# Linear attention and a cosine FFN on one core: the first 512 tokens taken from all four sequences instead of two

## The chip, the core and the metric

The kernel runs on one core of a Trainium2 chip. The core has a matmul engine (TensorE, PE in the profile), a vector engine (VectorE, DVE), an activation engine (ScalarE, ACT), a general engine (GpSimd, POOL) and a queue engine (SyncE, SP) that only issues DMAs. Sixteen DMA engines move data between the device memory and the core's on-chip memory. The metric is the device time of one execution in microseconds; lower is better. The profile shows one execution, and its span runs from the first to the last instruction.

## What is computed

For each of 4 sequences and 8 heads, with 768 tokens and head size 64, a linear attention with decay is computed in blocks of 64 tokens. Its output, 3072 tokens by 512, goes through an FFN with the gate h * cos(h):

```python
for b in range(nb):                                   # nb = 12 blocks of 64 tokens
    intra = einsum('bhic,bhjc->bhij', qb, kb) * Dmask
    intra = einsum('bhij,bhjd->bhid', intra, vb)
    inter = einsum('bhid,bhde->bhie', qb * lam_pow, kv_state)
    out[:, :, sl] = intra + inter
    kv_state = lam_block * kv_state + einsum('bhsd,bhse->bhde', kb * rev_pow, vb)
x = out.transpose(0, 2, 1, 3).reshape(3072, 512)
h = x @ w_in                                          # 512 x 2048
return (h * cos(h)) @ w_out                           # 2048 x 512
```

What matters below: the state of a sequence runs through its tokens in order, and different sequences have nothing to do with each other.

## The kernel before

**Blocks and pairs.** The 3072 tokens are 24 blocks of 128 (P). The function `where(n)` says which sequence and which chunk of it block n is. Two blocks of two sequences are worked on together as a pair. The first four blocks (SPANS = 2, so 2 * SPANS blocks) are special: a "span" x is 256 successive tokens of sequence x, that is its chunks 0 and 1. Token 2u + s lies on partition u with s beside it, so a span fills 128 partitions, chunk 0 the lower 64 of them (rows `halves[0]`) and chunk 1 the upper 64. After the spans come pairs 2 to 5 with chunks 2 to 5 of sequences 0 and 1, and pairs 6 to 11 with chunks 0 to 5 of sequences 2 and 3.

**A span (`add_span`).** Loads bring q and k as float32 by SP (`add_span_load`, tile `sp_f`) and v cast to bfloat16 by POOL (tile `v_sp`). `prep` scales q and k (DVE, for the second span's k POOL). TensorE transposes them, ACT copies the results out, TensorE forms the scores, DVE masks them (`scores_out`), and `values` multiplies with v. The second chunk of a span needs the state of the first: `update` (L631) makes it on TensorE, `update_out` copies it to `kv_bd` on ACT, and `carried` (L650) adds its part. `values_out` copies the attention output to `xT`, the input of the FFN. `add_span_state` (L705) then makes the state after both spans, 256 tokens, for pair 2: a PSUM result, a DVE copy (`sum`) and a POOL cast (`S`).

**A pair from 2 on.** `add_load` asks for q, k and v of both blocks (256 KB each, 1024 pieces of 256 bytes). POOL, DVE or ACT scale them (`prepare`). Up to pair 2 TensorE transposes; from pair 3 on (DMA_FROM = 6) SP issues two DMA transposes (L380). Then come scores (L422), update (L434), values (L484) and the part carried from the state (L516). A pair whose chunk is 0 has no carried part for its first half; the last pair of a group makes only one half of the update.

**The FFN (`add_ffn`).** Blocks are grouped in TILES of 4, 2, 2, 2, 2, 2, 2, 4 and 4. For each of the 16 slices of the hidden dimension there is a hidden matmul group (L738, 4 matmuls), a cosine on ACT (L744) and a product on DVE (L750, tile `g`). Then for each block four projection groups of four matmuls (L784) follow, a copy to `o_sb` and a store. A block of the first four stores its even and odd tokens apart, with two DMAs of 64 rows (L805); the others use one DMA of 128 rows (L807). All stores but the very last are on SP's queue.

**What sets the order.** `Planner.order` places every step by its assumed cost, its dependencies and a priority, and the instructions of each engine and queue are emitted in that order. Loads on SP follow the list `names`. Three links matter here. The load q of block 4, the first of pair 2 (the third pair), waits for the product of hidden slice KF - 3 = 13 of the first FFN tile (`pace`). The weights are loaded by POOL in pieces, w_in in six and w_out in four, the fourth w_out piece after q of block 4 has landed. And `keep_awake` puts idle matmuls into TensorE's gaps before the first FFN tile.

Of the kernel before, what the change touches and what calls it, by code (L numbers as in the profile page):

```python
# [10 lines left out]
F32 = mybir.dt.float32  # L11
BF16 = mybir.dt.bfloat16
# [6 lines left out]
SPANS = 2  # L19
# [15 lines left out]
STATE_OUT = [("ACT", "ACT"), ("ACT", "ACT")]  # L35
LATE = 30.0
ORDER = "q0 k0 q1 k1 v0 v1 i0 i1 i2 i3 i4 i5 o0 o1 o2 q4 q5 k4 k5 o3"

# [105 lines left out]
def kernel(  # L144
# [10 lines left out]
    nc = tc.nc  # L155
    B, H, S, D = q.shape
    P = 128
# [10 lines left out]
    def where(n):  # L168

        if n < 2 * SPANS:  # L170
            return n // 2, n % 2
        g, c = divmod(n // 2, NB)
        return 2 * g + n % 2, c

    BUFS = {"ld": 6, "qk": 3, "v_s": 6, "qkT": 3, "s_m": 4, "cos": 3, "o_sb": 4}
    ctx.enter_context(tc.manual_schedule())
# [6 lines left out]
    def bank(i, shape, dt, name):  # L183
        return psum.tile(shape, dt, tag=f"bank{i}", bufs=1, name=name)
# [6 lines left out]
    ident = consts.tile([P, P], BF16)  # L191
    make_identity(nc, ident)
    pos_sp = consts.tile([P, 2], F32)
    nc.gpsimd.iota(pos_sp, pattern=[[1, 2]], base=-S // 2, channel_multiplier=2,
                   allow_small_or_imprecise_dtypes=True)
    mask_sp = consts.tile([P, 2, P], F32)
    nc.gpsimd.memset(mask_sp, 1.0)
    for i in range(2):
# [10 lines left out]
    nc.vector.memset(halfpi, math.pi / 2.0)  # L209
    blank = consts.tile([P, 4 * P], F32)  # L210
    nc.vector.memset(blank, 0.0)  # L211
    kv_bd = consts.tile([P, 2, NP, P], BF16)
    nc.vector.memset(kv_bd, 0.0)
    lnl = consts.tile([P, H], F32)
    nc.scalar.activation(lnl, lam_bc, AF.Ln)
    expo_sp = consts.tile([P, H, 2], F32)
# [50 lines left out]
    def start(queue, o, x, deps):  # L267
        i = queue.dma_start(out=o, in_=x)  # L268
        for d in deps:
            tc.add_manual_dep(i.ins, d.issue.ins.ins.name, mybir.DependencyInfo(  # L270
                mybir.DependencyClass.Sync, mybir.DependencyReason.DATA), reason="order of loads")
        return i

    def add_span_load(name, src, x, prio, deps):
        def emit(_):
            if on_pool:
                t = span_v[x]
            else:
                if ("raw", x) not in live:
                    live["raw", x] = work.tile([P, 2, H, 2, D], F32, tag="g", name="sp_f")  # L280
                t = live[name, "sp", x] = live["raw", x][:, "qk".index(name[0])]
            return start(nc.gpsimd if on_pool else nc.sync, t.rearrange("u h s d -> u h (s d)"),
                         src[x, :, 0:2 * P, :].rearrange("h (u s) d -> u h (s d)", s=2), deps)

        on_pool = name == "v_f"
        issue, load_t[name, "sp", x] = dma("POOL" if on_pool else "SP", 1.5, 1.0 if on_pool else 0.5, emit, prio, deps,
                                           lat=0.95 if on_pool else 1.0)
        return load_t[name, "sp", x]

    def add_load(n, name, src, prio, deps=()):  # L290
        b, c = where(n)

# [10 lines left out]
        issue_t[name, n], load_t[name, n] = dma("SP", LOAD_US, 0.85, emit, prio, deps, get=name,  # L303
                                                lat=1.9 if name == "v_f" and n < 2 * SPANS + 2 else 1.0)
        return load_t[name, n]

    w_t, pace = {}, []
# [101 lines left out]
    def add_scores(pr, part):  # L409

        pa = lambda x: prio_attn(2 * pr, x)
        g, c = divmod(pr, NB)
        last, early = c == NB - 1, pr == SPANS
        nonlocal first_sum

# [57 lines left out]
    def add_stretch(pr):  # L473

        n0 = 2 * pr
        g, c = divmod(pr, NB)
        pa = lambda part: prio_attn(n0, part)
        tile_i, j0 = tile_of(n0)

# [96 lines left out]
        if (pr + 1, 1) in Uo:  # L576
            Uo[pr + 1, 1].deps.append(v2)
        for x, y in zip(chain, chain[1:]):
            x.then = y
# [5 lines left out]
    def add_span(x):  # L585
# [40 lines left out]
        def update(t):  # L626
            L["kv"] = bank(t.bank[0], [P, NP, P], F32, "ps_kv")
            rows = chunks[0][0]
            for p in range(NP):
                for s in range(2):  # L630
                    nc.tensor.matmul(L["kv"][:, p, :], lhsT=L["k"][rows, s, 2 * p:2 * p + 2, :], rhs=L["v"][rows, s, 2 * p:2 * p + 2, :],  # L631
                                     start=(p == 0 and s == 0), stop=True, skip_group_check=True)

        def update_out(_, h, e):
            (nc.scalar.copy if e == "ACT" else nc.vector.tensor_copy)(kv_bd[h, x, :, h], L["kv"][h, :, h])

        def values(task, hp):
            if hp == 0:
                L["o"] = [bank(i, [P, NP, P], F32, "ps_o") for i in task.bank]
            for p in range(2 * hp, 2 * hp + 2):  # L640
                for s in range(2):
                    for rows, c in chunks:
                        for i, h in enumerate(halves):
                            nc.tensor.matmul(L["o"][c][h, p, :], lhsT=L["v"][rows, s, 2 * p + i, :],  # L644
                                             rhs=L["s_m"][rows, i, p, s, :],
                                             start=(p == 0 and s == 0), stop=True, skip_group_check=True)

        def carried(_):
            for p in range(NP):
                nc.tensor.matmul(L["o"][1][:, p, :].rearrange("e (s u) -> e s u", s=2),  # L650
                                 lhsT=kv_bd[:, x, p, :], rhs=L["qT"][:, :, p, chunks[1][0]],
                                 start=False, stop=True, skip_group_check=True)

        def values_out(_, c, e):
            if ("xT", 0) not in live:
# [7 lines left out]
        for hp in range(2):  # L663
# [11 lines left out]
            s1 = pl.add("PE", 0.42, outs, partial(scores, hp=hp), pa(0.1 + 0.1 * hp), banks=2)  # L675
            if x and hp == 0:

                spans[0]["values"].deps.append(s1)
                s_first = s1
            so[hp] = [pl.add("DVE", 0.69, [s1], partial(scores_out, hp=hp, i=i), pa(0.1 + 0.1 * hp + 0.05 * i)) for i in range(2)]  # L680
            s1.bank_frees = [[t] for t in so[hp]]

        u = pl.add("PE", 0.42, v_t + kt + [spans[0].get("carried")], update, pv(0.1), banks=1)
        Uo_sp[x] = [pl.add(e, 0.4 if e == "ACT" else 0.42, [u], partial(update_out, h=h, e=e), pv(0.1))
                    for h, e in zip(halves, STATE_OUT[x])]
        u.bank_frees = [Uo_sp[x]]
        span_deps.extend(v_t + kt)
        v0 = pl.add("PE", 0.35, so[0] + v_t + [spans[0].get("carried")], partial(values, hp=0), pv(0.2), banks=2)
# [5 lines left out]
        L["update"], L["values"], L["carried"] = u, v0, second  # L694
        L["straight"] = v1

    def add_span_state():


        def update(t):  # L700
            live["kv", 1] = bank(t.bank[0], [P, H, D], F32, "ps_kv")
            for h in range(H):
                for s in range(2):
                    for L, r in zip(spans, halves):
                        nc.tensor.matmul(live["kv", 1][r, h, :], lhsT=L["k"][:, s, h, :], rhs=L["v"][:, s, h, :],  # L705
                                         start=(h == 0 and s == 0), stop=True, skip_group_check=True)

        def state(_):
            nc.vector.tensor_copy(new_sum(1, 1), live["kv", 1])  # L709

        def state_16(_):
            nc.gpsimd.tensor_copy(new_S(1, 1), live["sum", 1, 1])  # L712

        u = pl.add("PE", 16 * QUART + SW, span_deps + [w_t["out", 0]], update, LATE, banks=1)
        x = pl.add("DVE", 0.69, [u], state, LATE)
        Uo[1, 1] = pl.add("POOL", 0.61, [x], state_16, LATE)
        u.bank_frees = [[x]]

    h_last, o_last = {}, {}
    hid, closing = [], None  # L720
# [1 line left out]
    def add_ffn(i):  # L722
# [4 lines left out]
        for f in range(KF):  # L727
            gate[f] = []
            blocks = [(0, 2), (2, 4)] if i == 0 and f < SPLIT else [(0, nb)]
            for b0, b1 in blocks:  # L730
# [37 lines left out]
        for j in range(nb):  # L768
# [4 lines left out]
            for piece, part in enumerate(pieces):  # L773
# [26 lines left out]
                def store_out(_, eng, j=j, piece=piece, part=part, width=width):  # L800
                    b, c = where(n0 + j)
                    r0 = b * S + c * P
                    if n0 + j < 2 * SPANS:
                        for s, h in enumerate(halves):
                            nc.sync.dma_start(out=out[r0 + s:r0 + P:2, :], in_=live["o_sb", i, j, piece][h])  # L805
# [47 lines left out]
            pr += 1  # L853
        add_ffn(i)
    for f in range(2, SPLIT):
        hid[2 * f].deps.append(spans[1]["carried"])
    issue_t["q_f", 2 * SPANS].deps += pace
    closing.deps.append(v12[SPANS])
    first_sum.deps += Vo[2 * SPANS]
# [56 lines left out]
```

## Time and profile before

| | us |
|---|---|
| median of 3 runs | 204.16 (203.99 to 204.69) |
| the profiled execution | 204.18 |
| its span | 202.5 |
| TensorE busy | 193.8 |
| hidden matmuls (L738) | 90.5 |
| projection matmuls (L784) | 88.3 |
| TensorE's first hidden matmul starts at | 15.37 |
| TensorE's last matmul ends near | 199.6 |

The granted TensorE clock is full throughout. A mean of 168 GB/s goes through the DMA engines; the queue of SP takes 62.2% of the time of all sixteen, the queue of POOL 16.3%. The page's forty slices are of 5.06 us each. A digit in them is the busy share of a slice in tenths. In an "issue" row the time to landing counts from the issue.

The loads of q, k and v have a median of 3.9, 4.3 and 5.0 us to landing, a store of 256 KB 2.5 us, and a store of 128 KB (the halves of the first four blocks) 3.9 us.

### The profile page before, as it was taken

To read this page: it belongs to the slowest core of one execution; us is meant where nothing else is said; L and a number is where in the kernel's file an instruction comes from. 1 tells how busy PE (TensorE), PEld (TensorE's weight loads), DVE (VectorE), ACT (ScalarE), POOL (GpSimd) and SP (SyncE) were. 2 spreads that over 40 slices of the span, in tenths; PEclk is the share of its full clock that TensorE was granted. 3 is DMA by queue.
4 is the path that set the end of the run, shared out by engine and by line. 5 is a ranking of instruction groups with operands and counts; after the bars stand their busy time and mean duration, and the time that the engine had idled before them with its cause. 6 is when DMAs were issued, how large, how long until landed. Compare 5 with 4: busy or idle time off the path is not lost.

```text
span 202.5 us, 5913 instructions
## 1 busy us (share of the span) xinstructions
PE 193.8 (96%) x2441; PEld 116.4 (57%) x2469; DVE 116.6 (58%) x228; ACT 119.9 (59%) x240; POOL 64.7 (32%) x85
## 2 busy tenths in 40 slices
PE   6799999999999999999999999999999999999994
PEld 3367444547747858766658676755445444444443
DVE  2888774257954967858548575734579544444001
ACT  4978871228837878565639666654877554355120
POOL 5694004046245163544653272543510000000000
PEclk9999999999999999999999999999999999999999
DMA  4999999988889998999999999999920010111112
GB/s 117 324 189 206 202 204 217 184 191 217 188 212 239 241 217 195 229 157 254 254 254 186 237 236 154 256 146 273 234 68 3 3 52 0 52 55 52 52 52 104
DMA packets 96762, 33.94 MB, mean 168 GB/s; under 512 B 84320, under 2 KB 93792, under 8 KB 96736
## 3 DMA queue, kind: packets, MB, share of 16 engines
q1 hardware_dynamic: 89232, 28.78, 62.2%
q0 software_dynamic: 7360, 4.72, 16.3%
q8 instruction: 19, 0.31, 0.7%
q14 instruction: 7, 0.06, 0.1%
q10 hardware_dynamic: 144, 0.07, 0.1%
HBM read 27.27 MB, written 6.29 MB: 166 GB/s over the span
## 4 chain that ended last, share of the span: by engine, by line
PE 92%; DMA 3%; issue 2%; SPq 2%; POOL 1%; ACT 0%; POOLq 0%; ACTq 0%
PE ps_h L738 41%; PE ps_f L784 40%; DMA sp_f<-in_k_dram 3%; PE ps_o L484 2%; PE ps_s L422 2%; PE ps_kv L434 2%; PE ps_o L516 2%; SPq L268 1%; PE ps_o L644 1%; PE ps_kv L631 1%; POOL k_sp L599 1%; PE ps_x L484 0%; PE ps_t L374 0%; PE ps_t L607 0%; PE ps_s L618 0%
## 5 line engine op out<-in xcount | busy, mean ns | idle before, releaser
L750 DVE TENSOR_TENSOR g<-ps_h,cos 128x256 bf16<-128x256 f32 (+1 forms) x148 | 73.2, 503 | 42.9 <-ACT cos L744 42.0
L744 ACT ACTIVATE cos<-ps_h,halfpi 128x256 f32<-128x256 f32 (+1 forms) x148 | 75.7, 539 | 29.4 <-PE ps_h L738 28.6
L738 PE MATMUL ps_h<-xT,w_in_sb 128*128 128x256 bf16 (+1 forms) x586 | 90.5, 304 | 0.5 <-issue 0.3
L784 PE MATMUL ps_f<-w_out_sb,g 128*128 128x512 bf16 (+2 forms) x378 | 88.3, 370 | 2.0 <-issue 1.3
L738 PEld LDWEIGHTS <-w_in_sb 128*128 128x128 bf16 x592 | 57.1, 98 | 30.1 <-DVE xT L524 0.4
L784 PEld LDWEIGHTS <-g 128*128 128x128 bf16 x400 | 37.6, 98 | 37.2
L798 ACT COPY o_sb<-ps_f 128x512 f32<-128x512 f32 (+1 forms) x24 | 13.8, 573 | 29.7 <-PE ps_f L784 29.6
L344 POOL TENSOR_TENSOR qk<-q_f,q_scale 128x512 bf16<-128x512 f32 x19 | 19.6, 1045 | 36.4 <-DMA q_f<-in_q_dram 33.6
L352 POOL TENSOR_TENSOR v_s<-v_f,v_scale 128x512 bf16<-128x512 f32 x19 | 19.6, 1044 | 15.6 <-DMA v_f<-in_v_dram 12.6
L427 DVE TENSOR_TENSOR s_m<-ps_s,mask 128x512 bf16<-128x512 f32 x20 | 13.0, 685 | 3.6 <-PE ps_s L422 3.0
L348 POOL CAST qk<-k_f 128x512 bf16<-128x512 f32 x18 | 11.1, 614 | 11.0 <-DMA k_f<-in_k_dram 10.9
L524 ACT CAST xT<-ps_o 128x512 bf16<-128x512 f32 x11 | 6.0, 588 | 9.6 <-PE ps_o L516 6.3
L440 DVE TENSOR_TENSOR sum<-sum,ps_kv 128x512 f32<-128x512 f32 x15 | 10.2, 682 | 0.6
L445 ACT CAST S<-sum 128x512 bf16<-128x512 f32 x15 | 9.2, 617 | 0.9 <-DVE sum L440 0.8
L798 DVE COPY o_sb<-ps_f 128x384 f32<-128x384 f32 x1 | 0.6, 557 | 11.5 <-DMA out_dram<-o_sb 11.5
L484 PEld LDWEIGHTS <-v_s 64*64 64x64 bf16 x320 | 3.9, 107 | 4.1 <-issue 3.6
L876 PE MATMUL ps_idle<-blank 128*128 128x512 f32 (+2 forms) x8 | 4.7, 723 | 1.6 <-DVE blank L211 1.6
L623 DVE TENSOR_TENSOR s_m_sp<-ps_s,mask_sp 128x512 bf16<-128x512 f32 x8 | 5.1, 683 | 1.0 <-PE ps_s L618 1.0
L484 PE MATMUL ps_o<-s_m,v_s 64*64 64x64 bf16 x256 | 5.1, 196 | 0.1
L712 POOL CAST S<-sum 128x512 bf16<-128x512 f32 x1 | 0.6, 607 | 14.0 <-DVE sum L709 14.0
L501 DVE COPY spare<-ps_o 1x1 f32<-1x1 f32 x5 | 0.8, 156 | 7.3 <-PE ps_o L484 7.3
L535 DVE TENSOR_TENSOR xT<-ps_o,cross 128x256 bf16<-128x256 f32 x8 | 3.1, 422 | 2.9 <-PE ps_o L516 2.9
(74 smaller groups left out, 94.7 us busy)
## 6 DMA issues: line engine op xcount, KB each, us to landing
q_f<-in_q_dram SPq DMA_DIRECT2D x20, 256.0 KB, 3.9
k_f<-in_k_dram SPq DMA_DIRECT2D x20, 256.0 KB, 4.3
v_f<-in_v_dram SPq DMA_DIRECT2D x20, 256.0 KB, 5.0
out_dram<-o_sb SPq DMA_DIRECT2D x19, 256.0 KB, 2.5
w_out_sb<-in_moe_w_out_dram POOLq DMA_DIRECT2D x4, 512.0 KB, 12.8
sp_f<-in_q_dram SPq DMA_DIRECT2D x2, 512.0 KB, 6.2
sp_f<-in_k_dram SPq DMA_DIRECT2D x2, 512.0 KB, 5.6
w_in_sb<-in_moe_w_in_dram POOLq DMA_DIRECT2D x4, 256.0 KB, 6.9
```

What stands on the lines that cost most here:

```text
L344: vec[e].tensor_mul(new_qk()[:, 0, :, s], live.pop(("q_f", 2 * pr + s)), q_scale[:, c, :].unsqueeze(2).to_broadcast([P, H, D]))
L348: (nc.scalar.copy if early else nc.gpsimd.tensor_copy)(new_qk()[:, 1, :, s], live.pop(("k_f", 2 * pr + s)))
L352: vec[e].tensor_mul(live["v_s", 2 * pr + s], live.pop(("v_f", 2 * pr + s)), v_scale[:, c, :].unsqueeze(2).to_broadcast([P, H, D]))
L427: nc.vector.tensor_mul(t, live["s", pr][s], mask.unsqueeze(1).to_broadcast([P, H, D]))
L440: nc.vector.tensor_add(new, live["sum", pr, 0] if half else live["sum", pr - 1, 1], live["kv", pr][half])
L445: nc.scalar.copy(new_S(pr, half), live["sum", pr, half])
L484: yield lambda h=h: nc.tensor.matmul(o[halves[h % 2], h // 2], lhsT=live["v_s", n0 + s][m, h, :], rhs=live["s_m", n0 + s][m, h, :], start= ...
L738: nc.tensor.matmul(t[:, :n], lhsT=w_in_sb[:, kd, f * P:(f + 1) * P], rhs=live["xT", i][:, kd, at], start=(kd == 0), stop=(kd == KD - 1))
L744: nc.scalar.activation(c[:, :n], live["h", i, f, at.start][:, :n], AF.Sin, bias=halfpi)
L750: return nc.vector.tensor_mul(live["g", i][:, f, at], live.pop(("h", i, f, at.start))[:, :n], live.pop(("c", i, f, at.start))[:, :n])
L784: nc.tensor.matmul(live["f", i, j, piece][:, :width], lhsT=live["g", i][:, f, j * P:(j + 1) * P], rhs=w_out_sb[:, f, part], start=(f == 0) ...
L798: (nc.scalar.copy if eng == "ACT" else nc.vector.tensor_copy)(o[:, :width], live["f", i, j, piece][:, :width])
```

## The change

The first four blocks are now the first chunks of all four sequences. `where` gives blocks 0 to 3 the sequences 0, 1, 3 and 2 with chunk 0. A span's lower 64 partitions hold one sequence and its upper 64 another, so nothing is carried within a span: `update`, `update_out`, `carried` and `kv_bd` go. The span loads become two DMAs of 64 partitions each, as the halves now come from two sequences. `pos_sp` counts each half from the same position. `add_span_state` makes two states, one for each group of two sequences (keys 1 and 6), with 64 matmuls of 64 rows for 32 of 128. The pairs are then 2 to 6 with chunks 1 to 5 of sequences 0 and 1, and 7 to 11 with chunks 1 to 5 of sequences 2 and 3, so every pair has a carried part. The load of the third pair waits for hidden slice KF - 5 = 11. The planner's assumed latency for early v loads is 1.4 for 1.9. The store of a block of the first four is one DMA whose DRAM side is ordered by odd and even tokens first.

```diff
@@ where
         if n < 2 * SPANS:
-            return n // 2, n % 2
-        g, c = divmod(n // 2, NB)
+            return (0, 1, 3, 2)[n], 0
+        g, c = group(n // 2)
         return 2 * g + n % 2, c
+    def group(pr):
+        g, c = divmod(pr - SPANS, NB - 1)
+        return g, c + 1
...
-    nc.gpsimd.iota(pos_sp, pattern=[[1, 2]], base=-S // 2, channel_multiplier=2,
-                   allow_small_or_imprecise_dtypes=True)
+    for i in range(2):
+        nc.gpsimd.iota(pos_sp[i * D:(i + 1) * D], pattern=[[1, 2]], base=-S // 2, channel_multiplier=2,
+                       allow_small_or_imprecise_dtypes=True)
...
-    kv_bd = consts.tile([P, 2, NP, P], BF16)
-    nc.vector.memset(kv_bd, 0.0)
...
@@ add_span_load
-            return start(nc.gpsimd if on_pool else nc.sync, t.rearrange("u h s d -> u h (s d)"),
-                         src[x, :, 0:2 * P, :].rearrange("h (u s) d -> u h (s d)", s=2), deps)
+            for i, u in enumerate(halves):
+                last = start(nc.gpsimd if on_pool else nc.sync, t[u].rearrange("u h s d -> u h (s d)"),
+                             src[where(2 * x + i)[0], :, 0:P, :].rearrange("h (u s) d -> u h (s d)", s=2), () if i else deps)
+            return last
...
@@ add_span
-        u = pl.add("PE", 0.42, v_t + kt + [spans[0].get("carried")], update, pv(0.1), banks=1)
-        Uo_sp[x] = [pl.add(e, 0.4 if e == "ACT" else 0.42, [u], partial(update_out, h=h, e=e), pv(0.1))
-                    for h, e in zip(halves, STATE_OUT[x])]
-        u.bank_frees = [Uo_sp[x]]
...
-        second = pl.add("PE", MM(P, 4) + 0.1, [v1] + Uo_sp[x], carried, pv(0.3))
-        for c, (t, e) in enumerate(zip((v1, second), VALUES_OUT[x])):
-            Vo[2 * x + c] = [pl.add(e, 0.6 if e == "ACT" else 0.69, [t], partial(values_out, c=c, e=e), pv(0.3) if c == 0 else -1200.0)]
+        for c, e in enumerate(VALUES_OUT[x]):
+            Vo[2 * x + c] = [pl.add(e, 0.6 if e == "ACT" else 0.69, [v1], partial(values_out, c=c, e=e), pv(0.3) if c == 0 else -1200.0)]
...
@@ add_span_state
+        keys = [SPANS - 1, SPANS + NB - 2]
         def update(t):
-            live["kv", 1] = bank(t.bank[0], [P, H, D], F32, "ps_kv")
+            for key, i in zip(keys, t.bank):
+                live["kv", key] = bank(i, [P, H, D], F32, "ps_kv")
             for h in range(H):
                 for s in range(2):
-                    for L, r in zip(spans, halves):
-                        nc.tensor.matmul(live["kv", 1][r, h, :], lhsT=L["k"][:, s, h, :], rhs=L["v"][:, s, h, :],
-                                         start=(h == 0 and s == 0), stop=True, skip_group_check=True)
+                    for x, (key, L) in enumerate(zip(keys, spans)):
+                        for c, rows in enumerate(halves):
+                            nc.tensor.matmul(live["kv", key][halves[where(2 * x + c)[0] % 2], h, :],
+                                             lhsT=L["k"][rows, s, h, :], rhs=L["v"][rows, s, h, :],
+                                             start=(h == 0 and s == 0), stop=True, skip_group_check=True)
...
+        for i, key in enumerate(keys):
+            x = pl.add("DVE", 0.69, [u], partial(state, key=key), LATE + 2 * i)
+            Uo[key, 1] = pl.add("POOL", 0.61, [x], partial(state_16, key=key), LATE + 2 * i)
+            u.bank_frees.append([x])
...
@@ add_ffn
-                if i == 0 and f == KF - 3:
+                if i == 0 and f == KF - 5:
                     pace.append(d)
...
@@ store_out
                     if n0 + j < 2 * SPANS:
-                        for s, h in enumerate(halves):
-                            nc.sync.dma_start(out=out[r0 + s:r0 + P:2, :], in_=live["o_sb", i, j, piece][h])
+                        nc.sync.dma_start(out=out[r0:r0 + P, :].rearrange("(u s) m -> s u m", s=2),
+                                          in_=live["o_sb", i, j, piece])
                         return
```

More of the change, by code (lines that the diff above doesn't have):

```diff
@@ L34 @@
 VALUES_OUT = [("ACT", "ACT"), ("DVE", "ACT")]
-STATE_OUT = [("ACT", "ACT"), ("ACT", "ACT")]
 LATE = 30.0
@@ L303, in add_load @@
         issue_t[name, n], load_t[name, n] = dma("SP", LOAD_US, 0.85, emit, prio, deps, get=name,
-                                                lat=1.9 if name == "v_f" and n < 2 * SPANS + 2 else 1.0)
+                                                lat=1.4 if name == "v_f" and n < 2 * SPANS + 2 else 1.0)
         return load_t[name, n]
@@ L411, in add_scores @@
         pa = lambda x: prio_attn(2 * pr, x)
-        g, c = divmod(pr, NB)
+        g, c = group(pr)
         last, early = c == NB - 1, pr == SPANS
@@ L475, in add_stretch @@
         n0 = 2 * pr
-        g, c = divmod(pr, NB)
+        g, c = group(pr)
         pa = lambda part: prio_attn(n0, part)
@@ L575, in add_stretch @@
         qkT_head[pr].frees = [v2]
-        if (pr + 1, 1) in Uo:
+        if (pr + 1, 1) in Uo and group(pr + 1)[1] < NB - 1:
             Uo[pr + 1, 1].deps.append(v2)
@@ L624, in scores_out @@
                                         mask_sp.unsqueeze(1).to_broadcast([P, 2, 2, P]))
[L626 to L635, printed above, removed]
         def values(task, hp):
@@ L646, in values @@
                                              start=(p == 0 and s == 0), stop=True, skip_group_check=True)
[L648 to L652, printed above, removed]
         def values_out(_, c, e):
@@ L676, in add_span @@
             if x and hp == 0:
-                spans[0]["values"].deps.append(s1)
                 s_first = s1
@@ L681, in add_span @@
             s1.bank_frees = [[t] for t in so[hp]]
-        u = pl.add("PE", 0.42, v_t + kt + [spans[0].get("carried")], update, pv(0.1), banks=1)
-        Uo_sp[x] = [pl.add(e, 0.4 if e == "ACT" else 0.42, [u], partial(update_out, h=h, e=e), pv(0.1))
-                    for h, e in zip(halves, STATE_OUT[x])]
-        u.bank_frees = [Uo_sp[x]]
         span_deps.extend(v_t + kt)
-        v0 = pl.add("PE", 0.35, so[0] + v_t + [spans[0].get("carried")], partial(values, hp=0), pv(0.2), banks=2)
+        v0 = pl.add("PE", 0.35, so[0] + v_t, partial(values, hp=0), pv(0.2), banks=2)
@@ L693, in add_span @@
         v0.bank_frees = [Vo[2 * x], Vo[2 * x + 1]]
-        L["update"], L["values"], L["carried"] = u, v0, second
+        L["values"] = v0
         L["straight"] = v1
     def add_span_state():
+        keys = [SPANS - 1, SPANS + NB - 2]
         def update(t):
-            live["kv", 1] = bank(t.bank[0], [P, H, D], F32, "ps_kv")
+            for key, i in zip(keys, t.bank):
+                live["kv", key] = bank(i, [P, H, D], F32, "ps_kv")
             for h in range(H):
                 for s in range(2):
-                    for L, r in zip(spans, halves):
-                        nc.tensor.matmul(live["kv", 1][r, h, :], lhsT=L["k"][:, s, h, :], rhs=L["v"][:, s, h, :],
-                                         start=(h == 0 and s == 0), stop=True, skip_group_check=True)
@@ L708, in state @@
[L708 to L717, printed above, removed]
+                    for x, (key, L) in enumerate(zip(keys, spans)):
[3 more added lines that the diff above has]
+                                             start=(h == 0 and s == 0), stop=True, skip_group_check=True)
@@ new lines, in state, with state_16 @@
+        def state(_, key):
+            t = live["sum", key, 1] = toks.tile([P, H, D], F32, tag=f"first{key}", bufs=1, name="sum_first")
+            nc.vector.tensor_copy(t, live["kv", key])
+        def state_16(_, key):
+            t = live["S", key, 1] = toks.tile([P, H, D], BF16, tag=f"first16_{key}", bufs=1, name="S_first")
+            nc.gpsimd.tensor_copy(t, live["sum", key, 1])
+        u = pl.add("PE", 16 * QUART + SW, span_deps + [w_t["out", 0]], update, LATE, banks=2)
+        u.bank_frees = []
@@ L855 @@
     for f in range(2, SPLIT):
-        hid[2 * f].deps.append(spans[1]["carried"])
+        hid[2 * f].deps.append(spans[1]["straight"])
     issue_t["q_f", 2 * SPANS].deps += pace
```

## The prediction

> **What bounds the kernel now.** I read the page first (busy shares, slices, chain), then the chain in order of time, then the SP queue and the DMA traffic by window.
>
> ```profile
> PE 193.8 (96%) x2441; PEld 116.4 (57%) x2469; DVE 116.6 (58%) x228; ACT 119.9 (59%) x240; POOL 64.7 (32%) x85
> ...
> PE   6799999999999999999999999999999999999994
> ...
> DMA  4999999988889998999999999999920010111112
> ...
> PE 92%; DMA 3%; issue 2%; SPq 2%; POOL 1%; ACT 0%; POOLq 0%; ACTq 0%
> ```
>
> TensorE is the bound from the third slice (10 us) on: nothing but its own work and short issue gaps is on the chain from 11.35 to 199 us. But the DMA row is nearly as full up to slice 29 (147 us): the loads keep just ahead of TensorE. The chain in order of time (start, us, what) shows the lead and two places that matter later:
>
> ```profile
> 4.09 5.99 DMA sp_f<-in_k_dram
> 10.25 1.05 POOL k_sp L599
> ...
> 13.86 0.33 PE ps_o L650 x4
> 14.19 0.35 PE ps_s L618 x16
> 14.54 0.55 PE ps_kv L631 x8
> 15.09 0.35 PE ps_o L644 x16
> 15.44 0.98 PE ps_h L738 x8
> 16.41 0.35 PE ps_o L644 x16
> 16.76 0.33 PE ps_o L650 x4
> 17.09 2.40 PE ps_h L738 x21
> ...
> 56.27 0.38 PE ps_s L422 x32
> ...
> 69.60 0.38 PE ps_s L422 x32
> ```
>
> The update (L631) and carried (L650) rows go with the change. 56.27 and 69.60 are where TensorE needs the DMA transposes of pairs 3 and 4. The SP queue just before them:
>
> ```profile
> 43.80 2.29 SPq L268 DMA_DIRECT2D v_f<-in_v_dram  x2
> 46.19 4.13 SPq L805 DMA_DIRECT2D out_dram<-o_sb  x4
> 50.42 2.75 SPq L380 DMA_TRANSPOSE qkT<-qk  x2
> 53.22 0.58 SPq L268 DMA_DIRECT2D q_f<-in_q_dram  x1
> 53.89 1.17 SPq L805 DMA_DIRECT2D out_dram<-o_sb  x2
> ```
>
> The two transposes stand behind the first stores; the second is issued at 51.8 and, at 2.8 us to landing, lands near 54.6, 1.6 us before 56.27. That is all the slack there. Last, what one packet costs: DMA traffic in 194.0 to 194.5, where only one store runs (queue: packets, MB, share of 16 engines):
>
> ```profile
> q1 hardware_dynamic: 74, 0.15, 77.1%
> ```
>
> 0.771 x 16 x 0.5 us / 74 = 83 ns for a 2 KB packet. In 46 to 47, where loads run, 935 packets take 104.0%: 17.8 ns each.
>
> [...]v_f is issued at 35.29, yet in 36.5 to 38.5 only q0's weights move.[...]
>
> **The change part by part.**
>
> *Lead.* Both updates and both carried steps go, and ACT's four kv_bd copies (0.37 each) with them. Of TensorE's pieces on the chain between 13.86 and 17.09, 0.33 + 0.55 + 0.33 are removed. What is late next: POOL. v_sp becomes four issues. 1024-descriptor ones took 1.08 and 0.89 us, the 512-descriptor w_in ones 0.77; four at 0.77 are 3.1 for 1.96, so 1.1 more before the two w_in issues, and POOL's cover is its 0.97 idle before k_sp. k_sp starts about 0.15 later. From there: key transposes, copies, scores and masks run 0.1 later than before; the hidden x8 then waits only for ACT's two xT copies, behind the last kT copy, near 15.3 (15.44 before); values end at 16.6 and hidden goes on there instead of at 17.09. Gain 0.45, taken. Bounds: 0.2 (split loads land later; SP issues eight for four, within its time before 5.5) to 0.75 (POOL not late). The next w_in chunk with little slack lands at 13.04 + 7.5 = 20.5 (issue and landing by window) and is used from 21.2 before (ten slices of 4 x 217 ns ahead of 29.86, where the last one ends), so a gain over 0.6 ends there.
>
> *TensorE afterwards.* Pair 6 was a first pair with 16 carried matmuls (0.16 us); the first pair of the second group now has 32 (0.32 to 0.34): +0.16. The state step has 64 matmuls of 64x64 for 32 of 128x64 (0.69): 32 scores of that tile took 0.26 to 0.38, so 0.52 to 0.76; taken as no change. All other rows keep their number; last pairs stay two.
>
> *Nothing on the path.* kv_bd's memset (DVE 0.48), one more iota (POOL 0.13), one more DVE copy (0.69) and POOL cast (0.61): DVE waits 1.1 and POOL 1.5 there for q_f. If that cover went they would cost their own length at 33 us, where the transposes at 35.98 still have room.
>
> *Third pair's loads two slices sooner.* Two slices are 8 matmuls of 217 ns: 1.7 us. POOL's weights fill the engines until about 30.5, so q_f gains about 0.7 only. v_f, its POOL product and the update at 44.26, which now comes four projections earlier, gain alike. Worth nothing: no wait stood there. If cover went, 0 to 1.6 (rival 3).
>
> *The store.* `(u s) m -> s u m` makes one DMA of two, with slowest sizes 2 on the DRAM side and 128 on the other.[...] Then 256 KB lie on two engines: 64 packets x 83 ns = 5.4 us each, where sixteen needed 0.67. SP saves four issues of about 1 us, but everything behind a store on those two engines waits, loads and transposes being spread over all. Their work, in SP's order in the changed kernel: store 0, store 1, two transposes (pair 3), a load, store 2, a load, store 3, four loads, an ordinary store, two transposes (pair 4). A load is 64 packets x 17.8 ns = 1.1; a transpose 1.4 (2.75 for two). Start: when pair 3's v_f has passed, 43.80 + 4.4 = 48.2 before, now about 47.8.
> - Pair 3: 47.8 + 2 x 5.4 + 2 x 1.4 = 61.4; needed at 56.27 - 0.45 = 55.8. Stall 5.6.
> - Pair 4: 61.4 + 2 x 5.4 + 6 x 1.1 + 0.7 + 2 x 1.4 = 82.3; needed at 69.60 - 0.45 = 69.15 without a stall. Stall 13.2 in all (the first within it).
> - Pair 5: one more round of 6.6 + 1.4 + 2.8 = 10.8 ends at 93.1; needed at 81.18 - 0.45 + 13.2 = 93.9. It has caught up; pair 6 is even or a few tenths late.
>
> Price bounds: [...]at 7 us, if loads on the other engines slow the packets by a third, 19.6. I take 5.4, measured on an undisturbed store.
>
> **Sum** against the profiled run: span 202.5, 1.7 around it, 204.18 in all (median shown 204.16). -0.45 + 0.16 + 13.2 = +12.9, hence 217.1 us.
>
> **Rivals.** (1) Not slower: the store still runs on sixteen engines[...]. Place: the four stores from 46 us; price 0.67 us each[...]. Then -0.45 + 0.16 = -0.3: 203.9.[...] (2) Two engines, but later transfers do not queue behind the stores (transposes and loads hardly delayed): only a remainder of the slack is lost, 204 to 207, say 205.5.[...] (3) Stores harmless, but the sooner q_f holds up the last w_out third loaded early (16.7 + 15.5 = 32.2), which the fourth projection group needs at 30.70 + 3 x 0.87 = 33.3 before and 32.8 now[...] against: q1 waited for q0 at 36.5.
>
> **How the numbers follow.** Two-engine stall 0.82, rival (1) 0.11, (2) 0.04, (3) 0.03. 0.3% (0.6 us) is what a measurement can tell from no change. Rival (1) around 203.9 gives 0.05 faster, 0.05 same, 0.01 slower; with small shares of (2) and (3), faster 0.06, same 0.06, slower 0.88. The range takes the price bounds of the likeliest:[...] 210.5 to 224.
>
> **What would show it.** DMA row: a stretch from 48 to 82 with much lower share and rate than before; the L794 stores with about 6 to 12 us to landing for 256 KB (2.5 for ordinary ones); TensorE idle before the scores of pairs 3 and 4 of about 5.6 and 7.6 us; hidden going on near 16.6; loads and transposes even again by 95 us. Wrong if those stores land in under 4 us, or TensorE stays at nine tenths in all slices.

## The result

The changed kernel takes 222.21 us (median of 6 runs, 221.43 to 222.7), the kernel before 204.26 beside it: 1.087 times as long, 95% interval 1.0842 to 1.0898. The profiled execution has a span of 220.4 us, 17.9 more than before. The forecast was 217.1 in a range of 210.5 to 224; the upper end is an estimate from stores of 7 us (the price of 5.4 with packets slowed by a third), the lower one was the author's estimate and rests on no measured price. Executions more than 1.5% above the fastest of their kernel are left out of the ratios below, which concerns two of the four with outermost size 4 and one of the six with the old pace.

The page of the changed kernel, busy shares and slices (5.5 us each):

```profile
PE 200.2 (91%) x2467; PEld 118.8 (54%) x2495; DVE 116.1 (53%) x228; ACT 118.4 (54%) x236; POOL 66.4 (30%) x89
...
PE   7799999999819964999999999999999999999994
...
PEclk9999999999967995899999999999999999999999
DMA  4999999996963569999899999994990001110212
```

Two holes have come into TensorE's row, at slices 11 and 15 (counted from 0, so near 60 to 66 and 80 to 88 us). The DMA row falls to 3 to 6 tenths around the first one. New too is the clock row: it falls to 6 and 5 tenths at and after the holes, where it was full throughout before. The view of waits names what ended the holes (total, times, longest):

```profile
PE ps_s L427 <- DMA qkT<-qk: 10.4, 2, 5.6
...
PE ps_h L728 <- DMA w_in_sb<-in_moe_w_in_dram: 0.4, 1, 0.4
```

These are the scores of pairs 3 and 4, waiting for their DMA transposes: 5.60 us before 65.52 and 4.75 before 85.24 by the timeline. SP's queue there (start, length of the issue, kind):

```profile
50.09 1.53 SPq L794 DMA_DIRECT2D out_dram<-o_sb  x2
51.71 11.77 SPq L385 DMA_TRANSPOSE qkT<-qk  x2
63.53 0.58 SPq L271 DMA_DIRECT2D q_f<-in_q_dram  x1
64.22 0.55 SPq L794 DMA_DIRECT2D out_dram<-o_sb  x1
64.82 0.55 SPq L271 DMA_DIRECT2D q_f<-in_q_dram  x1
65.46 3.36 SPq L794 DMA_DIRECT2D out_dram<-o_sb  x1
68.88 4.36 SPq L271 DMA_DIRECT2D k_f<-in_k_dram  x2
```

The two transposes behind the two stores hold SP for 11.77 us, where before they took 2.75; so everything behind them is also issued later, not only moved later. What the engines do meanwhile, DMA traffic from 58 to 63 us (queue: packets, MB, share of 16 engines):

```profile
q1 hardware_dynamic: 126, 0.26, 13.1%
```

0.131 x 16 is 2.1, so by this share two of sixteen engines are busy. 0.131 x 16 x 5 us / 126 gives 83 ns for a packet of 2 KB, the price that the prediction took from before.

Where the 17.9 us come in, by stage. First the kernel before, from the scores of pair 2 to those of 3, 3 to 4 and 4 to 5; then the changed kernel between the same marks (window, length and TensorE busy, then the other engines, clock, DMA share, GB/s):

```profile
40.33:56.27 15.94, 15.42 (x228) 10.43 (x236) 11.16 (x23) 9.84 (x22) 6.39 (x7) 1.00 0.87 206
56.27:69.60 13.33, 13.01 (x219) 9.37 (x224) 8.72 (x19) 9.43 (x22) 5.40 (x6) 1.00 0.96 222
69.60:81.20 11.60, 11.34 (x204) 7.81 (x209) 8.55 (x20) 8.44 (x20) 5.32 (x6) 1.00 0.95 210
```

```profile
44.77:65.52 20.75, 14.70 (x218) 10.05 (x221) 11.05 (x23) 9.84 (x22) 6.39 (x7) 0.92 0.94 139
65.52:85.24 19.72, 14.47 (x210) 9.96 (x212) 9.24 (x20) 9.94 (x23) 5.40 (x6) 0.85 0.63 156
85.24:98.80 13.56, 13.13 (x197) 8.65 (x204) 8.07 (x18) 7.93 (x18) 5.43 (x7) 0.84 1.00 220
```

The three stages cost 4.8, 6.4 and 2.0 us more. In the third there is no wait at all: TensorE is busy 13.1 us for 11.3 because of its clock, 0.84. What is left of the 17.9 lies ahead of them: pair 2's scores come at 44.77 for 40.33, 4.4 later; 0.8 of it is a projection group that now stands ahead of them and no longer behind, and 3.6 is the lead, since the state step starts at 33.64 for 30.00. From pair 5 to the end it is 121.6 for 121.3.

The lead, in the chain of waits (start, us, what):

```profile
6.67 7.12 DMA sp_f<-in_k_dram
...
14.02 2.04 POOL k_sp L604 x2
16.07 0.74 POOL w_in_sb L271
16.80 8.05 DMA w_in_sb<-in_moe_w_in_dram
...
24.90 5.37 PE ps_h L728 x24
```

The last k of the spans lands at 13.79, before at 10.07; POOL's scaling of it starts at 14.02 for 10.25, and the first hidden group at 18.59 for 15.37. SP had issued that load at 6.67, so the wait is in the transfer. DMA traffic from 4 to 8 us, before and after:

```profile
q1 hardware_dynamic: 2746, 1.38, 114.8%
```

```profile
q1 hardware_dynamic: 1977, 0.98, 116.8%
```

The engines are as full as before, but a packet of 512 bytes takes 1.168 x 16 x 4 us / 1977 = 38 ns for 27, and so 246 GB/s flow for 346. The loads onto 64 partitions are slower by themselves.

### The profile page after: what moved, and what is told of

Its sections match the earlier page's. It is cut to its first block, busy times and chain, and to the rows that moved or that the text cites. A ratio compares the mean times of both kernels' runs of the same rounds, so it can differ in the third digit from the quotient of the medians.

```text
span 220.4 us, 5967 instructions
## 1 busy us (share of the span) xinstructions
PE 200.2 (91%) x2467; PEld 118.8 (54%) x2495; DVE 116.1 (53%) x228; ACT 118.4 (54%) x236; POOL 66.4 (30%) x89
## 3 DMA queue, kind: packets, MB, share of 16 engines
q0 software_dynamic: 7392, 4.72, 15.4%
## 4 chain that ended last, share of the span: by engine, by line
PE 62%; DMA 17%; SPq 15%; POOL 2%; issue 2%; ACT 0%; DVE 0%; POOLq 0%; ACTq 0%
PE ps_h L728 28%; PE ps_f L774 28%; SPq L271 10%; DMA v_f<-in_v_dram 6%; SPq L385 4%; DMA w_in_sb<-in_moe_w_in_dram 4%; DMA sp_f<-in_k_dram 3%; DMA k_f<-in_k_dram 3%; SPq L794 2%; DMA qkT<-qk 2%; PE ps_o L521 1%; PE ps_s L427 1%; PE ps_o L489 1%; PE ps_kv L439 1%; POOL k_sp L604 1%
## 5 line engine op out<-in xcount | busy, mean ns | idle before, releaser
L774 PE MATMUL ps_f<-w_out_sb,g 128*128 128x512 bf16 (+2 forms) x378 | 90.1, 377 | 2.1 <-issue 1.5
L774 PEld LDWEIGHTS <-g 128*128 128x128 bf16 x400 | 38.3, 99 | 39.6 <-issue 2.7
L357 POOL TENSOR_TENSOR v_s<-v_f,v_scale 128x512 bf16<-128x512 f32 x19 | 19.7, 1043 | 14.8 <-DMA v_f<-in_v_dram 14.3
L353 POOL CAST qk<-k_f 128x512 bf16<-128x512 f32 x18 | 11.0, 614 | 12.8 <-DMA k_f<-in_k_dram 12.8
L427 PE MATMUL ps_s<-qkT 64*64 64x64 bf16 x320 | 4.8, 203 | 10.4 <-DMA qkT<-qk 10.4
L427 PEld LDWEIGHTS <-qkT 64*64 64x64 bf16 x320 | 3.7, 116 | 12.2 <-DMA qkT<-qk 11.1
L445 DVE TENSOR_TENSOR sum<-sum,ps_kv 128x512 f32<-128x512 f32 x14 | 9.5, 681 | 0.7
L866 PE MATMUL ps_idle<-blank 128*128 128x512 f32 (+2 forms) x8 | 5.8, 885 | 1.6 <-DVE blank L216 1.6
L700 POOL CAST S_first<-sum_first 128x512 bf16<-128x512 f32 x2 | 1.2, 614 | 14.5 <-DVE sum_first L696 14.5
## 6 DMA issues: line engine op xcount, KB each, us to landing
w_out_sb<-in_moe_w_out_dram POOLq DMA_DIRECT2D x4, 512.0 KB, 13.2
```

Of the source, the lines that this page charges most:

```text
L353: (nc.scalar.copy if early else nc.gpsimd.tensor_copy)(new_qk()[:, 1, :, s], live.pop(("k_f", 2 * pr + s)))
L357: vec[e].tensor_mul(live["v_s", 2 * pr + s], live.pop(("v_f", 2 * pr + s)), v_scale[:, c, :].unsqueeze(2).to_broadcast([P, H, D]))
L427: nc.tensor.matmul(live["s", pr][s][m, h, :], lhsT=kT[r, h, m], rhs=qT[r, h, m], start=True, stop=True, skip_group_check=True)
L445: nc.vector.tensor_add(new, live["sum", pr, 0] if half else live["sum", pr - 1, 1], live["kv", pr][half])
L774: nc.tensor.matmul(live["f", i, j, piece][:, :width], lhsT=live["g", i][:, f, j * P:(j + 1) * P], rhs=w_out_sb[:, f, part], start=(f == 0) ...
```

## The experiments

Each result is a ratio to the kernel before, timed beside it on the same chip.

**The store, taken out of the change and put into the kernel before.** First the changed kernel with the old stores:

```diff
-                        nc.sync.dma_start(out=out[r0:r0 + P, :].rearrange("(u s) m -> s u m", s=2),
-                                          in_=live["o_sb", i, j, piece])
+                        for s, h in enumerate(halves):
+                            nc.sync.dma_start(out=out[r0 + s:r0 + P:2, :], in_=live["o_sb", i, j, piece][h])
```

> The changed kernel with the old stores of the first four blocks (two DMAs of 64 rows each). Theory A (the one-DMA store runs on two engines; the loads and transposes behind it stall TensorE twice, 5.6 + 4.75 us, and each stall leaves the TensorE clock at half for some 4 us): both stalls and the half clock go, 222.2 - 10.4 - 3.6 = 208.2 us (207 to 209), and the 3.6 us of the later lead stay. Theory B (the transposes are late because the whole queue order of loads is later by the lead and the new third pair): stalls stay, 218 or more.

Measured: 207.52 us, 1.0147 (1.0123 to 1.0172). No wait for a transpose is left. The other way round, the edit reversed in the kernel before:

> The kernel before with the one-DMA store alone. Theory A: in the changed kernel pair 3's scores start 15.4 us after the first such store is issued; here that is 46.2 + 15.4 = 61.6 against 56.3 needed, a stall of 5.3, then one of about 4.7, and half clock behind each, 3.6 in all: 204.2 + 13.6 = 217.8 us (215 to 220). Theory B: 204 to 206.

Measured: 218.28 us, 1.069 (1.0634 to 1.0747). Its waits:

```profile
PE ps_s L422 <- DMA qkT<-qk: 10.9, 2, 6.7
```

The store alone makes both holes. It costs 13.9 us in the kernel before and 222.2 - 207.5 = 14.7 in the changed one; the rest of the change costs 207.5 - 204.4 = 3.1, against the kernel before beside it. Of the 14.7, some 0.8 lies ahead of the stores, in the lead of the two profiled executions (state step at 33.64 for 32.88 with the old stores); the stages from the first hole on make 14.0.

**Is it the outermost size?** The same single DMA, but with its DRAM side ordered by 4 or by 16 instead of 2. In these two kernels the rows of the first four blocks come out in another order than the reference's; bytes and number of DMAs are those of the changed kernel.

```diff
-                        nc.sync.dma_start(out=out[r0:r0 + P, :].rearrange("(u s) m -> s u m", s=2),
+                        nc.sync.dma_start(out=out[r0:r0 + P, :].rearrange("(u s) m -> s u m", s=4),
```

> The changed kernel with the outermost size of the one-DMA store's DRAM side 4 in place of 2 (rows of a block written in another order, so the order of rows in the first four blocks' output is not the reference's; bytes and DMA count are the same). Theory K (the outermost size is the number of engines): four engines, 2.7 us a store; pair 3's transposes are there 5.4 us sooner, 60.1 against 59.9 needed: 207.5 to 208.5 us. Rival (the order of rows on the DRAM side, or one DMA in place of two, makes the store slow): 220 or more.

> As before with outermost size 16 (rows again in another order than the reference's). Theory K: all sixteen engines, as fast as the old two DMAs: no stall, 207 to 207.7 us. Rival: 220 or more.

Measured: a median of 215.12 us with 4 (its four runs spread from 211.84 to 215.73; 1.0441, 1.0342 to 1.0541) and 208.59 with 16 (1.0206, 1.0147 to 1.0265). DMA traffic with 4 from 58 to 60 us, where nearly all packets are stores, and with 16 from 53 to 54 us, where smaller packets run beside them:

```profile
q1 hardware_dynamic: 54, 0.11, 22.1%
```

```profile
DMA packets 260, 0.35 MB, mean 346 GB/s; under 512 B 105, under 2 KB 105, under 8 KB 259
q1 hardware_dynamic: 259, 0.34, 103.0%
```

0.221 x 16 = 3.5 engines with 4. With 16 all sixteen are busy; 154 of the packets are of 2 KB, and at 83 ns each they alone need 154 x 83 ns / 1 us = 12.8 engines (an estimate from the price above). So in these three kernels the engines at work went with the outermost size (2.1 for 2, 3.5 for 4, all sixteen for 16), and neither the order of rows nor the single DMA is to blame: with 16 the time is that of the old stores within the intervals. It came 0.9 us above what was expected; the third pair's scores already start 1.3 us later than with the old stores (45.3 for 44.0), so that lies ahead of the stores. The size of the middle point was missed too. With four engines, in the profiled execution (215.73 us, the slowest of the four), a 2 KB packet takes 0.221 x 16 x 2 us / 54 = 131 ns and not 83, so twice the engines moved only 58 GB/s for 51, and stalls of 3.9 and 0.9 us stayed. Why four engines are slower apiece no run here shows.

**The lead: narrow loads or more DMAs?** Two versions of the kernel before, each with two DMAs for every span load: one split by partitions, one by heads.

```diff
@@ split by partitions
+            for i, u in enumerate(halves):
+                last = start(nc.gpsimd if on_pool else nc.sync, t[u].rearrange("u h s d -> u h (s d)"),
+                             src[x, :, i * P:(i + 1) * P, :].rearrange("h (u s) d -> u h (s d)", s=2), () if i else deps)
@@ split by heads
+            for i in range(2):
+                g = slice(4 * i, 4 * i + 4)
+                last = start(nc.gpsimd if on_pool else nc.sync, t[:, g].rearrange("u h s d -> u h (s d)"),
+                             src[x, g, 0:2 * P, :].rearrange("h (u s) d -> u h (s d)", s=2), () if i else deps)
```

> The kernel before with each span load (q, k, v) made as two DMAs of 64 partitions each. Theory P (a DMA onto 64 partitions runs at about 240 GB/s where one onto 128 runs at 345): the last k of the spans lands 3.7 us later, near 13.8, and the first hidden matmul starts near 18.6: 204.2 + 3.6 = 207.8 us (207 to 208.5). Theory Q (the lead is later because SP and POOL issue twice as many DMAs): also 207.8, so this one is to be read beside the split by heads. Neither: 204.2.

> The kernel before with each span load made as two DMAs of four heads each, both onto all 128 partitions: as many DMAs as in the split by 64 partitions. Theory P: loads keep their rate of about 345 GB/s, first hidden matmul at 15.4 to 15.9, 204.2 to 204.7 us. Theory Q: as late as the split by 64 partitions, 207.8 us.

Measured: 210.17 us split by partitions (1.0249, 1.0199 to 1.0299), 205.21 split by heads (1.0047, 1.0026 to 1.0067). DMA traffic from 4 to 8 us, by partitions and by heads:

```profile
q1 hardware_dynamic: 2019, 1.00, 115.2%
```

```profile
q1 hardware_dynamic: 2684, 1.33, 113.3%
```

As many DMAs in both, 251 GB/s in the one, 333 in the other. It is the split by partitions. Whether it is the 64 partitions on the chip's side, or the other order in which each DMA then reads the device memory, no run separates. The number of DMAs costs what is left, 0.8 us here, of which 0.35 is seen at POOL: its four v issues end later, and k_sp starts at 10.60 for 10.25. The split by partitions came out 2.4 us above what was expected. In its profiled execution (210.53 us, 6.3 longer than that of the kernel before, where the fastest run took 208.46) the first hidden group starts 3.9 us later than before, at 19.24, and behind it TensorE waits 0.5 us for a product of POOL, 0.5 for a transpose, 0.3 for a w_in chunk and 0.2 for a product of DVE, none of which it waited for before; what is left, some 0.9, is not placed.

**Do two queues bring the rate back?** The changed kernel with the old stores, the lower halves issued by SP, the upper ones by ACT ahead of its first activation:

```diff
+    raw = [work.tile([P, 2, H, 2, D], F32, tag="g", name="sp_f") for _ in range(2)]
+    for x in range(2):
+        for i, a in enumerate((q, k)):
+            nc.scalar.dma_start(out=raw[x][D:P, i].rearrange("u h s d -> u h (s d)"),
+                                in_=a[where(2 * x + 1)[0], :, 0:P, :].rearrange("h (u s) d -> u h (s d)", s=2))
```

> The changed kernel with the old stores, and the lower halves (64 partitions) of the spans' q and k loads issued by SP, the upper halves at the same time by ACT's queue. Theory P1 (64 partitions are slow[...]): 345 GB/s again, hidden starts near 15.0 to 15.5, 203.9 to 204.6 us. Theory P2[...]: loads keep 240 GB/s, 207.0 to 208 us.

Measured: 207.77 us, 1.0148 (1.0119 to 1.0177), no better than from one queue. Both queues share the engines from 4 to 8 us:

```profile
q10 hardware_dynamic: 1053, 0.52, 60.6%
q1 hardware_dynamic: 1041, 0.52, 55.5%
```

A packet still takes 1.161 x 16 x 4 us / 2094 = 35 ns, and 260 GB/s flow for 247 from one queue in the same window, 5% more. In this trace the two queues ran side by side, at 60.6% and 55.5% of the engines. The first hidden group did start earlier, at 17.25 for 18.45 with one queue, but a w_in chunk is then waited for 0.7 us; at the state step 0.3 of the gain is left (32.60 for 32.88), at the scores of pair 3 nothing (59.13 for 59.10).

**The change without its narrow loads.** The old stores and the old span loads, each one DMA onto 128 partitions from one sequence; the rest is the changed kernel. It reads tokens 128 to 255 of two sequences in place of the first chunks of the other two, so what is computed from these is not the reference's.

> The changed kernel with the old stores, and each span load made as one DMA onto 128 partitions from one sequence, as before. It reads tokens 128 to 255 of two sequences in place of the first chunks of the other two, so its first blocks and what follows from them are not the reference's; the work on each engine is that of the changed kernel. It prices the lead without the slow loads: the prediction's terms alone give 204.4 - 0.45 + 0.16 = 204.1 us, hidden from about 15.3 and going on at 16.6. If the lead has another cost than the loads, 205 or more; if the two removed steps are worth all their TensorE time, 203.3.

Measured: 204.02 us, 0.9978 (0.9965 to 0.9992). Its timeline on TensorE where the lead ends (start, us, what):

```profile
14.87 1.03 PE L726 MATMUL ps_h<-xT,w_in_sb 128*128 128x256 bf16 x8
15.83 0.42 PE L636 MATMUL ps_o<-s_m_sp,v_sp 64*64 64x128 bf16 x16
16.18 2.07 PE L726 MATMUL ps_h<-xT,w_in_sb 128*128 128x256 bf16 x17
...
55.77 0.45 PE L425 MATMUL ps_s<-qkT 64*64 64x64 bf16 x32
```

Hidden goes on at 16.18 for 16.93 in the same view of before, the scores of pair 3 start at 55.77 for 56.20, 0.43 sooner. This is the gain for which two sequential steps were taken out of the lead: 0.3 us in the end, if the loads were as fast as they were. The narrow loads, two DMAs of 64 partitions for one of 128, in turn cost 207.52 - 204.02 = 3.5 us; in the kernel before they cost 5.8, with the further waits named above.

**The third pair's loads.** The changed kernel with the old stores and the old pace:

```diff
-                if i == 0 and f == KF - 5:
+                if i == 0 and f == KF - 3:
```

> The changed kernel with the old stores, and the third pair's q load waiting for hidden slice 13 again. The prediction put the sooner loads at nothing: 207.5 us, within 0.4 of the version with slice 11. If the sooner loads were worth what two slices last: 209.2.

Measured: 207.7 us, 1.017 (1.0124 to 1.0216), not to be told from slice 11. q_f is issued at 31.89 for 30.98, and TensorE does not wait for what is made of it.

**What is the slow clock worth?** Idle matmuls put into the two stalls:

```diff
             qT, kT = live["qkT", pr][:, 0], live["qkT", pr][:, 1]
+            for _ in range({3: 20, 4: 20}.get(pr, 0)):
+                nc.tensor.matmul(live["s", pr][0].rearrange("p h d -> p (h d)"), lhsT=blank[:, :P], rhs=blank,
+                                 start=True, stop=True, skip_group_check=True)
```

> The changed kernel with 20 idle matmuls of 512 columns (4.3 us at full clock) placed before the scores of pairs 3 and 4, inside the two stalls of 5.6 and 4.75 us. Theory C (the idle itself halves the clock, and the work behind the stalls pays for it): clock full throughout, the scores start when they did, and the time falls by 3.2 to 3.6, to 218.6 to 219.0 us. Rival (the clock falls for another reason, or the slower matmuls behind the stalls are waits on something else): 222 or more.

Measured: 242.7 us, 1.1866 (1.181 to 1.1921). The fill was too long: `blank` is float32, and 20 such matmuls take 17.33 us by the timeline, not 4.3, so they overran the stalls. Still it can be read: 2 x 17.3 of filling less 10.4 of stalls would add 24.2, and 20.5 came, 3.7 less, while the clock was full (a mean of 1.00). By the timeline TensorE is 1.7 us faster from the scores of pair 3 to the end of what stands before those of pair 4 (13.2 for 15.0 us), and 1.9 from there to those of pair 5 (11.6 for 13.5). With 5 in place of 20:

> The changed kernel with 5 idle matmuls of 512 float32 columns (0.86 us each by the run with 20 of them, 4.3 us in all) before the scores of pairs 3 and 4, inside the stalls of 5.6 and 4.75 us. Theory C (idle alone halves the clock): clock full throughout, time down by 3.2 to 3.6, 218.6 to 219.0 us. Rival: 222 or more.

Measured: 221.4 us, 1.0818 (1.0776 to 1.086); against the changed kernel's 1.0842 to 1.0898 the intervals overlap. TensorE's timeline (the fill, then the scores of pairs 3, 4 and 5, with the idle time before them and what ended it):

```profile
60.05 4.46 PE L425 MATMUL ps_s<-blank 128*128 128x512 f32 x10
67.21 0.45 PE L430 MATMUL ps_s<-qkT 64*64 64x64 bf16 x32 [2.71 <-DMA qkT<-qk]
...
80.44 4.46 PE L425 MATMUL ps_s<-blank 128*128 128x512 f32 x10
85.80 0.44 PE L430 MATMUL ps_s<-qkT 64*64 64x64 bf16 x32 [0.90 <-DMA qkT<-qk]
...
98.45 0.45 PE L430 MATMUL ps_s<-qkT 64*64 64x64 bf16 x32 [1.00 <-DMA qkT<-qk]
```

The clock stays full (1.00 from 60 to 98.4 us) and scores take 0.45 us again for 0.64, so here it was the idle time that had halved it, as theory C had it. But the gain of 3.2 to 3.6 did not come. TensorE again needs only 13.2 us from the scores of pair 3 to the hole of pair 4, yet those of pair 4 start no sooner, at 85.80 for 85.24: they start when their transposes land, and a faster TensorE only waits longer, 5.4 us with the fill for 4.75. In the changed kernel, too, what ended last before pair 4's scores was a v load from 73.28, POOL's scaling of it and the transpose from 81.81, with no TensorE work among them. So the half clock behind pair 3 had cost nothing. Behind pair 4 the 1.9 us that TensorE gains are halved, as pair 5 too now waits for its transpose, 1.00 us: from pair 4 to pair 5 it is 12.65 us for 13.52. What is left, 0.9, agrees with the 0.8 measured (221.4 for 222.2). In the run with 20, where the DMAs had time to catch up, the whole 3.7 showed. Pair 3's transposes landed 1.7 us later than in the changed kernel, with the first store issued only 0.2 later; why is not known. The lead was slow too, its first hidden group at 19.49 for 18.59, with the clock at 0.50 from 11.6 to 18.4 us (a mean of 0.82 from 0 to 19).

A half clock in the lead, where TensorE waits for the loads, shows in the pages of four of the profiled executions with narrow loads (slices of 5 or 7 tenths, between 8.7 and 18.4 us), but not in the changed kernel's own (9 tenths there), so it is no part of its account. With the old stores, executions with it and without took the same, 207.2 to 207.9.

No version here that computes the reference beats the kernel before.

## Why the prediction came out as it did

**The store (right in mechanism, +13.2 forecast, 13.9 and 14.7 measured).** That an outer size of 2 puts a store on two engines was the author's assumption when the forecast was made. It holds: 2.1 engines busy, 83 ns a packet, and the outermost sizes of 4 and 16 gave 3.5 and sixteen. That the transposes are spread over all engines shows in the kernel before, where from 51.7 to 53 us, with hardly a packet of anything else, they take 90.0% of the sixteen. Pair 3's stall was put at 5.6 and is 5.60, partly by luck: the first store was issued at 50.1 and not at 47.8, the transposes came 15.4 us after it and not 13.6, and the need came at 59.9 and not at 55.8; the first two errors cancel the third. Pair 4's was put at 7.6 and is 4.75: TensorE itself took 1.6 us longer between the two at its lower clock and so asked later, and the transposes came 19.7 us after pair 3's and not 20.9. That the sum still comes near, 14.0 by stages for 13.2, is luck in part: the 2.0 behind pair 4 stood in no term. "It has caught up at pair 5" is right as far as waits go, none there, but only because TensorE was slow; at full clock it waited 1.0.

**The clock (missing).** No term stood for it. Windows of the changed kernel (clock third from the end):

```profile
60.00:62.00 2.00, 0.00 (x0) 0.00 (x0) 0.00 (x0) 0.00 (x0) 0.00 (x0) 1.00 0.13 51
62.00:64.00 2.00, 0.00 (x0) 0.00 (x0) 0.00 (x0) 0.00 (x0) 0.00 (x0) 0.56 0.49 117
...
67.00:69.00 2.00, 2.00 (x5) 0.69 (x5) 1.78 (x3) 0.00 (x0) 1.02 (x1) 0.50 0.43 102
69.00:71.00 2.00, 2.00 (x10) 0.88 (x9) 0.00 (x0) 1.30 (x3) 0.00 (x0) 0.98 0.13 51
```

Windows of half a microsecond place the changes: down at 62.23, 2.3 us after TensorE's last matmul, and up at 69.06, 3.5 us after work resumed; at the second hole down at 82.72, after 2.2 us, and up at 89.54, after 4.3. Neighbouring changes lie 6.83, 13.66 and 6.82 us apart. In the kernel before with the single store the clock was 0.84 in the mean from 57 to 63 us and 0.86 from 75 to 84, so it went down near 61.1 and 81.5, after some 4.7 and 2.9 us of idle (estimates from these means). In the split by partitions the half clock of the lead lasted 3.44 us (0.95, 0.50 and 0.69 from 8 to 14 us in windows of 2), and the three distances above are about twice, four times and twice that. Why one hole was at half clock after 2.2 us and another only after 4.7 no run here shows. A hole of 3.9 us brought it too (outermost size 4, 6 tenths in that slice), 2.71 us of idle did not (the run with five idle matmuls, 1.00).

A forecast of a stall of this length has to carry it, but not at its full length. TensorE's work took 1.6 us longer between the holes and 2.0 behind the second; the first was hidden, as pair 4's transposes were the later ones, and of the second 1.0 would have been a wait. What the clock itself cost is then about 1 us, an estimate; the run with five idle matmuls came out 0.8 faster, with intervals that overlap.

**The lead (the step that failed: forecast -0.45 with a worst case of -0.2, measured +3.1 with what else the change brings; the narrow loads alone cost 3.5).** The working priced the split by its issues alone: "split loads land later; SP issues eight for four, within its time before 5.5". SP's eight issues ended at 7.36 in fact, and that was not the point; the term of the sum that was wrong is the transfer itself, taken at the rate of 128 partitions. At 246 GB/s for 346 the 2 MB of q and k take 8.5 us for 6.1, and the share that overlaps v lengthens too: the last k lands 3.7 us later. That POOL would come "about 0.15 later" through four v issues held in kind, 0.35 in the split by heads; in the changed kernel it vanished behind 3.21 us that POOL waited for k. With the loads as before, the same working gives 204.2 - 0.45 + 0.16 = 203.9, and 204.02 was measured.

**Nothing on the path, sooner loads at nothing, TensorE afterwards +0.16.** The first two held: no wait for the added iota, copies or casts appears, and the old pace made no difference. The third was not tried alone; from pair 5 to the end the changed kernel takes 0.3 more.

**The rivals.** (1) fell by the 2.1 busy engines and a store of 83 ns a packet on them. (2) fell because the transposes did wait, 15.4 us from the first store to the scores of pair 3. (3), a starved weight chunk, showed in small and elsewhere: 0.4 us for a w_in chunk at 24.90, through the late lead and not through q_f.

The forecast came out 5.1 us low: 3.5 from the loads, 1.5 from the store with the clock behind its stalls (14.7 for 13.2).

## What to carry to other kernels

Before a DMA is split or merged, look at two sizes: the outermost size of its patterns, which set how many engines worked here (2.1, 3.5 and sixteen for 2, 4 and 16), and how many partitions it covers, since two of 64 moved 246 GB/s where one of 128 moved 346, and 260 from two queues. The store on two engines held up what stood behind it in the queue as well as what waited for it: two transposes held SP for 11.77 us where they had taken 2.75. And TensorE's stalls of 5.60 and 4.75 us brought 3.5 and 4.3 us of work at half clock behind them, the first hidden behind the same late DMAs, the second about 1 us on top, an estimate.

## What was not expected of the hardware

Four engines storing 2 KB rows took 131 ns a packet where two took 83, so doubling the engines raised the rate from 51 to only 58 GB/s, in one profiled execution. Two DMA transposes behind the stores held SP itself for 11.77 us (2.75 with the old stores, 9.75 with outermost size 4, 3.85 with 16), so that a late transfer became late issues for loads that had nothing to do with it. And the changes of TensorE's clock lay 6.83 or 13.66 us apart in the changed kernel's execution; one hole was at half clock after 2.2 us, another, in the kernel before with the single store, only after some 4.7.
